# Reordering the opening of a state-space block fused with a gated feed-forward: inputs ahead of weights, own products ahead of the weight decoding

## The chip, the cores and the metric

The kernel runs on one core of a Trainium2 chip. The metric is the time of one execution on the device, in microseconds. A core has a matrix engine (TensorE, PE in the profile; the loading of its stationary operand is listed apart as PEld), a vector engine (VectorE, DVE), an activation engine (ScalarE, ACT), a general engine (GpSimd, POOL) and a sync engine (SyncE, SP) that in this kernel issues every DMA transfer. Each engine runs its own instructions in the order of the program and waits on semaphores for the others. Instructions of the matrix engine write to PSUM[...]; every bank is a named buffer that has to be free before it is written again.

## What is computed

Two stages. The first is a chunked state-space recurrence for 4 batches and 8 heads, 768 steps, head width 32, state width 16; the second a feed-forward with a hard-swish gate on the 3072 rows of 256 values that the first leaves.

```python
# first stage, per batch and head, per chunk of steps (cum is the running sum of log a)
L   = exp(cum[i] - cum[j])  for i >= j, else 0
M   = (C @ B.T) * L
y   = M @ x  +  (C @ state) * exp(cum)
state = exp(cum[last]) * state + sum_j B[j] x[j].T * exp(cum[last] - cum[j])
# second stage
h = y @ w_in                     # 256 -> 2048
g = h * clip(h + 3, 0, 6) / 6
out = g @ w_out                  # 2048 -> 256
```

The kernel works through six blocks (chunks) of 128 steps, each with 4 x 128 = 512 rows. The weights arrive as double precision (64 bits) and are decoded on the chip into float32: they come in eight pieces of 1 MB, four of w_in and four of w_out, numbered 0 to 7 as raws[i].

## The kernel before: the parts that the change touches

The decoding of one piece is a generator; each `weights(i, n)` advances it by n steps. The line numbers of the profile are put beside the operations.

```python
def decode(i):
    ...
    nc.scalar.copy(out=s, in_=top)                     # L199 ACT: sign and exponent bits
    def significand():
        nc.vector.tensor_scalar(out=m, in0=hi, ...)    # L202 DVE
        yield
        nc.vector.scalar_tensor_tensor(out=m, in0=lo, in1=m, ...)  # L206 DVE
        yield
    parts_m = significand()
    if i < 2:
        next(parts_m)
        next(parts_m)
    yield
    nc.vector.tensor_scalar(out=e, in0=s, ...)         # L216 DVE
    nc.vector.tensor_scalar(out=s, in0=s, ...)         # L218 DVE
    next(parts_m, None)
    yield
    nc.scalar.activation(e, e, AF.Relu, bias=bias_hi, ...)   # L222 ACT
    yield
    nc.scalar.activation(e, e, AF.Relu, bias=bias_lo, ...)   # L224 ACT
    next(parts_m, None)
    if i and i + NRAW < 2 * NP:
        load_w(i + NRAW)
    yield
    nc.vector.tensor_tensor(out=e, in0=e, in1=s, op=ALU.bitwise_or)  # L229 DVE
    nc.vector.scalar_tensor_tensor(out=dst, in0=m, in1=e, ...)       # L237 DVE: writes w_in or w_out
```

The steps of the first stage, cut to what is moved:

```python
def diff_mask(c, b):   # L337 PE: starts the differences of chunk c, batch b with the causal mask
def diff(c, *bs):      # L349 and L358 PE: adds cum[i] - cum[j]
def diff_exp(c, b):    # L366 ACT: L = exp(differences)
def turn_b(c):         # L423 PE: four transposes of B, then an ACT copy (L432) to bT
def ends(c, b):        # L397 POOL: B times the decay to the end of the chunk
def scores(c):
    ...                # banks cb0 to cb3 (tags f0 to f3) and y0, y1
    for b in range(NB):            # L523 PE, 64 products: cb <- C, B
        ...
    into_state(c, 0, 1)            # L535 PE, 64 products: y banks <- x, B (what goes into the state)
def multiply(c):
    take(c)                        # L551 ACT: adds <- y
    if c == 0:
        ...                        # L559 ACT, twice: mid <- y (the state in the middle of the chunk)
    for q in range(NQ):
        ...                        # L564 DVE, four times: L <- L * cb[q]
def mix(c):
    for u in range(2):
        ...                        # L589 PE, 64 products: y <- L, x (own products)
        if c == 0:
            from_state(c, 1, ...)  # L501 PE, 16 products: y <- C, mid (from the state)
def keep(c):                       # L603 ACT, four times: yT <- y
def mlp_in(k, f):                  # L611 PE: h <- yT, w_in ; then L689 ACT, L694 DVE
def busy(n, bank):                 # L491 PE: n products of the identity, whose result nobody reads
```

The opening in order of the program:

```python
    load_w(0)
    load_bc(0)      # C in eight transfers of 256-byte runs, then B in one of 64-byte runs
    load_x(0)
    ...
    for c in range(2):
        for b in range(NB):
            diff_mask(c, b)
    ...
    in_three()                       # L277 to L281 DVE: cum split in three bfloat16 parts
    for b in range(2):
        mask_again(0, b)             # L344 PE: 128x512, only to fill the wait
    diff(0, 0, 1)
    diff(0, 2, 3)
    turn_squares(bcs[0][0], turned(0)[2])   # L466 DVE: C turned
    part_heads(0)                           # L473 DVE, twice
    for b in range(NB):
        diff_exp(0, b)
    first_eto()                             # L372 PE, L377 ACT
    weights(0, 1)
    add_up(ends_at[1])                      # L270 DVE
    store_rows()
    diff(1, 2, 3)
    turn_b(0)
    for b in range(NB):
        ends(0, b)
    weights(0, 1)
    diff(1, 0, 1)
    diff_exp(1, 2)
    diff_exp(1, 3)
    weights(0, 2)
    scores(0)
    multiply(0)
    load_w(1, behind=Ls[0][:, 0, 2, :1])    # waits until L <- L * cb[1] is done
    load_w(2)
    load_w(3)
    c_ps = ...; turn_cum(c_ps); by_token(c_ps)
    busy(1, ...)
    fade(0, HALF[1])                        # L479 DVE
    weights(0, 1)
    mix(0)
    keep(0)
    weights(1, 2)
    renew(0)
    weights(1, 3)
    load_eto(1)
    load(1)
    ...
    for f in range(NF):                     # block 0, first product
        mlp_in(k, f)
        for i in weave.get(f, []):
            weights(i, 1)
        if f in (6, 8):
            diff_exp(c, f // 2 - 3)
```

Of the kernel before, what the change touches and what calls it, by code (L numbers as in the profile page):

```python
# [8 lines left out]
FP32 = mybir.dt.float32  # L9
# [4 lines left out]
ALU = mybir.AluOpType  # L14
# [6 lines left out]
def kernel(  # L21
# [63 lines left out]
    def load_bc(c):  # L85

        sl = slice(c * P, (c + 1) * P)

        def tokens_first(src, **where):
            t = loads.tile([P, NB * NH, N], FP32, **where)
            nc.sync.dma_start(out=t, in_=src[:, :, sl, :].rearrange("b h s n -> s (b h) n"))
            return t

        def pairs_first(src):
            t = loads.tile([P, 2, NB, 4, N], FP32, name="pairs", tag="bc")
            for b in range(NB):
                for h in range(2):
                    nc.sync.dma_start(  # L100
                        out=t[:, h, b].rearrange("s a n -> s (a n)"),
                        in_=src[b, h:NH:2, sl, :].rearrange("h (s a) n -> h s (a n)", a=4))
            return t

        if c == 0:
            bcs[c] = [pairs_first(C)]
        elif c < TURN:
            bcs[c] = [tokens_first(C, name="C", tag="bc")]
        Bs[c] = tokens_first(B, name="B")
        if c < TURN:  # L110
            bcs[c].append(Bs[c])
        else:
            bcs[c] = [pairs_first(C), pairs_first(B)]

    def load_x(c):
        sl = slice(c * P, (c + 1) * P)
        xts[c] = loads.tile([P, NB * NH, D], FP32, name="xt")
        nc.sync.dma_start(out=xts[c], in_=x[:, :, sl, :].rearrange("b h s d -> s (b h) d"))
# [22 lines left out]
        nc.sync.dma_start(out=dst, in_=src)  # L141
        raws[i] = raw

    load_w(0)
    load_bc(0)
    load_x(0)
    nc.scalar.preload_act_table_set("natural_log_exp_and_others")


# [38 lines left out]
    def decode(i):  # L188
# [20 lines left out]
            yield  # L209

        parts_m = significand()
        if i < 2:
            next(parts_m)
            next(parts_m)
        yield
# [1 line left out]
            out=e, in0=s, scalar1=0x7FF0, scalar2=None, op0=ALU.bitwise_and)  # L217
        nc.vector.tensor_scalar(  # L218
            out=s, in0=s, scalar1=0x8000, scalar2=None, op0=ALU.bitwise_and)
        next(parts_m, None)  # L220
        yield
        nc.scalar.activation(e.bitcast(BF16), e, AF.Relu, bias=bias_hi, scale=-8.0)  # L222
        yield
        nc.scalar.activation(e, e.bitcast(BF16), AF.Relu, bias=bias_lo, scale=-1.0)  # L224
        next(parts_m, None)
        if i and i + NRAW < 2 * NP:
            load_w(i + NRAW)
        yield
# [110 lines left out]
            start=True, stop=True)  # L339
        ds[c, b] = d  # L340

    def mask_again(c, b):

        nc.tensor.matmul(  # L344
            out=ds[c, b], lhsT=ident_h, rhs=hide.unsqueeze(1).to_broadcast([P, NH, HT]),
            start=True, stop=True)

    def diff_less(c, b):
        nc.tensor.matmul(  # L349
# [64 lines left out]

    def turn_ps(c, j):

        if c < 2:
            return ps.tile([P, NB, P], FP32, name="t_ps", tag=f"f{2 * j if c else 1}")
        return ps_o.tile([P, NB, P], FP32, name="t_ps", tag="o")

    def transposes(c, j, t_ps):
# [23 lines left out]

    def fade_c(c, t_ps):

        nc.vector.tensor_tensor(out=turned(c)[2], in0=t_ps, in1=etos[c], op=ALU.mult)

    def turn(c, j):  # L450
        if j:
# [9 lines left out]
        for b in range(NB):  # L461
            ends(c, b)

    def turn_squares(t, out):

        nc.vector.transpose(  # L466
            out=out.rearrange("r b (s a) -> r b a s", a=4),
            in_=t.rearrange("s t b a n -> s (b a) t n"))

    def part_heads(c):  # L470
        _, cT, csT = turned(c)
        for t in range(2):
            nc.vector.tensor_scalar(  # L473
                out=cT[:, :, t], in0=csT, scalar1=parity[:, t:t + 1], scalar2=None,
                op0=ALU.mult)

    def fade(c, sl=slice(0, P)):
        csT = turned(c)[2][:, :, sl]
        nc.vector.tensor_tensor(out=csT, in0=csT, in1=etos[c][:, :, sl], op=ALU.mult)  # L479

    def turn_all(c):
        bT, _, csT = turned(c)
        for t, out_ in zip(bcs[c], (csT, bT)):
            turn_squares(t, out_)
        part_heads(c)
        fade(c)

    def busy(n, bank):

# [16 lines left out]
    def scores(c):  # L506

        bT, cT, _ = bTs[c]
        cbs[c] = [ps.tile([P, NB, 2, HT], FP32, name="cb", tag=f"f{q}") for q in range(NQ)]
        both = [ps_y.tile([P, 2, NB, HT], FP32, name=f"y{u}", tag=f"y{u}") for u in range(2)]
        ys[c] = {(0, u): both[u][:, 0] for u in range(2)}
        sps[c] = [both[a if c else 1 - a][:, 1] for a in range(2)]
        if c:
            from_state(c, 0)
        for b in range(NB):
            for a, rows in enumerate(HALF):  # L520
                for q in range(NQ):
                    pair = slice(32 * q, 32 * q + 32)
                    nc.tensor.matmul(  # L523
                        out=cbs[c][q][rows, b], lhsT=bT[pair, b, rows],
                        rhs=cT[pair, b, :, rows], start=(b == 0), stop=True,
                        tile_position=(32 * q, a * HT), skip_group_check=True)
        into_state(c, 0, 1)

    def into_state(c, *halves):
        xt, bs = xts[c], bss[c]  # L530
# [22 lines left out]
    def multiply(c):  # L553

        take(c)
        mids[c] = mid = att.tile([P, NB, 2 * D], FP32, name="mid", bufs=1)
        if c == 0:
            for t in range(2):
                nc.scalar.activation(  # L559
                    mid[:, :, t * D:(t + 1) * D], sps[c][0][:, :, t * D:(t + 1) * D], AF.Copy,  # L560
                    scale=parity[:, t:t + 1])
        for q in range(NQ):
            hs = slice(2 * q, 2 * q + 2)
            nc.vector.tensor_tensor(  # L564
                out=Ls[c][:, :, hs], in0=Ls[c][:, :, hs], in1=cbs[c][q], op=ALU.mult)
            if c and q == 1:
                new_state(mid, sps[c][0], tmps[c])

    def renew(c):

# [277 lines left out]
            for b in bs:  # L848
                part(c, b)

    for c in range(2):
        for b in range(NB):
            diff_mask(c, b)
    for sl in ends_at:
        log_a(sl)
    row_signs()
    add_up(ends_at[0])
    in_three()
    for b in range(2):
        mask_again(0, b)  # L860
    diff(0, 0, 1)
    diff(0, 2, 3)
    turn_squares(bcs[0][0], turned(0)[2])
    part_heads(0)
    for b in range(NB):
        diff_exp(0, b)
    first_eto()
    weights(0, 1)
    add_up(ends_at[1])
    store_rows()  # L870
    diff(1, 2, 3)
    turn_b(0)
    for b in range(NB):
        ends(0, b)
    weights(0, 1)
    diff(1, 0, 1)
    diff_exp(1, 2)
    diff_exp(1, 3)
    weights(0, 2)
    scores(0)  # L880
    multiply(0)
    load_w(1, behind=Ls[0][:, 0, 2, :1])
    load_w(2)
    load_w(3)
    c_ps = ps.tile([P, NC, G], FP32, name="c_ps", tag="f1")
    turn_cum(c_ps)
    by_token(c_ps)
    busy(1, ps.tile([P, NB * P], FP32, name="d", tag="f0"))
    fade(0, HALF[1])
    weights(0, 1)  # L890
    mix(0)
    keep(0)
    weights(1, 2)
    renew(0)
# [10 lines left out]
    for k in range(NC):  # L905
        gTs[k] = ffn.tile([P, NF, TB], FP32, name="gT")
        c, ahead = k + 1, k + 2
        if k == 0:
            for f in range(NF):
                mlp_in(k, f)  # L910
                for i in weave.get(f, []):
                    weights(i, 1)
                if f in (6, 8):
                    diff_exp(c, f // 2 - 3)
            load(ahead)
# [119 lines left out]
```

## Time and profile before

| | before |
|---|---|
| median of three runs | 362.05 us (361.94 to 362.84) |
| span of the profiled execution | 361.1 us |
| PE busy | 349.9 us, 97% of the span |
| DVE busy | 223.3 us, 62% |
| ACT busy | 177.2 us, 49% |
| POOL busy | 139.5 us, 39% |
| mean granted clock of PE | 0.989 of full speed |

The busy shares say that the matrix engine is the engine that the whole kernel leans on: what shortens the time has to take away idle or slow time of PE, or work from it. The shares are means over the span, though, and the change touches only the first 40 us or so. That stretch has to be read by itself: from the order of time of the instructions, from the stretches with their granted PE clock, and from the chain of what released what.

### The profile page before, as it was taken

To read this page: it belongs to the slowest core of one execution; us is meant where nothing else is said; L and a number is where in the kernel's file an instruction comes from. 1 tells how busy PE (TensorE), PEld (TensorE's weight loads), DVE (VectorE), ACT (ScalarE), POOL (GpSimd) and SP (SyncE) were. 2 spreads that over 40 slices of the span, in tenths; PEclk is the share of its full clock that TensorE was granted. 3 is DMA by queue.
4 is the path that set the end of the run, shared out by engine and by line. 5 is a ranking of instruction groups with operands and counts; after the bars stand their busy time and mean duration, and the time that the engine had idled before them with its cause. 6 is when DMAs were issued, how large, how long until landed. Compare 5 with 4: busy or idle time off the path is not lost.

```text
span 361.1 us, 9354 instructions
## 1 busy us (share of the span) xinstructions
PE 349.9 (97%) x3936; PEld 300.4 (83%) x3936; DVE 223.3 (62%) x427; ACT 177.2 (49%) x390; POOL 139.5 (39%) x139
## 2 busy tenths in 40 slices
PE   7698999999999999999999999999999999999996
PEld 3553438888888999888999888999888999888996
DVE  4778999976787634587435587535588421588111
ACT  4548878439656550575460476470476110476100
POOL 3400000182299712079722079720058700058700
PEclk9699999999999999999999999999999999999999
DMA  5979969901935043560034560000000000000000
GB/s 154 109 270 254 145 230 156 172 2 43 181 55 77 4 98 91 72 93 2 2 76 104 79 96 2 4 2 31 29 2 1 4 2 31 30 3 0 2 29 31
DMA packets 75482, 24.97 MB, mean 69 GB/s; under 512 B 66032, under 2 KB 71824, under 8 KB 74928
## 3 DMA queue, kind: packets, MB, share of 16 engines
q1 hardware_dynamic: 75440, 24.37, 34.7%
q8 instruction: 31, 0.51, 0.6%
q14 instruction: 11, 0.09, 0.1%
HBM read 21.07 MB, written 3.29 MB: 67 GB/s over the span
## 4 chain that ended last, share of the span: by engine, by line
PE 76%; DVE 13%; ACT 4%; DMA 3%; SPq 2%; issue 1%; DVEq 0%; POOL 0%; ACTq 0%
PE ob L767 18%; PE even L653 18%; PE oa L767 18%; PE odd L653 13%; DVE gT L694 2%; DVE wm L206 2%; PE o L708 2%; PE y L589 2%; PE cb L523 2%; PE y L501 2%; ACT we L222 2%; SPq L100 2%; DMA raw<-in_moe_w_in_dram 2%; DMA B<-in_B_dram 1%; DVE w_out L237 1%; DVE we L229 1%
## 5 line engine op out<-in xcount | busy, mean ns | idle before, releaser
L753 POOL TENSOR_TENSOR s<-gT 128x512 f32<-128x512 f32 x20 | 26.4, 1321 | 89.5 <-DVE gT L694 89.5
L653 PE MATMUL even<-ts,w_sum 128*128 128x256 f32 x160 | 48.2, 383 | 0.0
L668 ACT COPY even<-odd 128x512 f32<-128x512 f32 x40 | 23.0, 576 | 48.6 <-PE odd L653 46.3
L689 ACT ACTIVATE gT<-odd,half 128x512 f32<-128x512 f32 x40 | 27.5, 687 | 35.0 <-DVE odd L682 35.0
L653 PE MATMUL odd<-yT,w_in 128*128 128x256 f32 x160 | 41.1, 379 | 0.0
L767 PE MATMUL oa<-w_out,gT 128*128 128x128 f32 x320 | 38.9, 277 | 0.0
L767 PEld LDWEIGHTS oa<-w_out,gT 128*128 128x128 f32 x320 | 38.1, 192 | 0.9
L767 PE MATMUL ob<-w_out,s 128*128 128x128 f32 x320 | 37.4, 275 | 0.0
L767 PEld LDWEIGHTS ob<-w_out,s 128*128 128x128 f32 x320 | 36.5, 192 | 0.0
L653 PEld LDWEIGHTS even<-ts,w_sum 128*128 128x128 f32 x160 | 29.9, 190 | 5.3 <-ACT up L675 1.5
L694 DVE SCALAR_TENSOR_TENSOR gT<-gT,odd 128x512 f32<-128x512 f32 x40 | 27.5, 688 | 9.9 <-ACT gT L689 9.9
L653 PEld LDWEIGHTS odd<-yT,w_in 128*128 128x128 f32 x160 | 30.1, 190 | 3.9
L386 ACT ACTIVATE L<-L,cum_n 128x64 f32<-128x64 f32 x128 | 31.1, 339 | 0.0
L767 PE MATMUL ob<-t,gT 128*128 128x128 f32 x240 | 30.3, 279 | 0.0
L611 PE MATMUL h<-yT,w_in 128*128 128x512 f32 x64 | 28.4, 599 | 1.9 <-DVE gT L694 1.6
L689 ACT ACTIVATE gT<-even,half 128x512 f32<-128x512 f32 x40 | 27.7, 694 | 4.4 <-PE even L653 4.4
L694 DVE SCALAR_TENSOR_TENSOR gT<-gT,even 128x512 f32<-128x512 f32 x40 | 27.1, 679 | 4.4 <-ACT gT L689 4.4
L767 PEld LDWEIGHTS ob<-t,gT 128*128 128x128 f32 x240 | 27.9, 192 | 1.2 <-issue 0.5
L708 PE MATMUL o<-w_out,gT 128*128 128x256 f32 x128 | 28.7, 381 | 0.0
L669 DVE COPY up<-odd 128x256 f32<-128x256 f32 x40 | 17.0, 424 | 18.7 <-ACT even L668 17.9
L708 PEld LDWEIGHTS o<-w_out,gT 128*128 128x128 f32 x128 | 24.0, 190 | 4.0 <-ACT gT L689 0.8
L397 POOL TENSOR_TENSOR bs<-B,L 128x128 f32<-128x128 f32 x24 | 14.5, 612 | 31.6 <-ACT L L386 23.5
(130 smaller groups left out, 614.9 us busy)
## 6 DMA issues: line engine op xcount, KB each, us to landing
raw<-in_moe_w_in_dram SPq DMA_DIRECT2D x4, 1024.0 KB
raw<-in_moe_w_out_dram SPq DMA_DIRECT2D x4, 1024.0 KB
L<-cum_d SPq DMA_DIRECT2D x8, 512.0 KB
xt<-in_x_dram SPq DMA_DIRECT2D x6, 512.0 KB
out_dram<-res SPq DMA_DIRECT2D x20, 128.0 KB
B<-in_B_dram SPq DMA_DIRECT2D x6, 256.0 KB
eto<-cum_e SPq DMA_DIRECT2D x20, 64.0 KB
pairs<-in_C_dram SPq DMA_DIRECT2D x32, 32.0 KB
```

The source lines that it names most:

```text
L100: nc.sync.dma_start(out=t[:, h, b].rearrange("s a n -> s (a n)"), in_=src[b, h:NH:2, sl, :].rearrange("h (s a) n -> h s (a n)", a=4))
L386: nc.scalar.activation(Ls[c][:, b, h], Ls[c][:, b, h], AF.Exp, bias=cum_n[:, c, g:g + 1])
L397: nc.gpsimd.tensor_tensor(out=bss[c][:, hs], in0=Bs[c][:, hs], in1=Ls[c][:, b, :, HT - 1:HT].to_broadcast([P, NH, N]), op=ALU.mult)
L611: nc.tensor.matmul(out=h.rearrange("p r i -> p (r i)"), lhsT=w_in[:, j, f * P:(f + 1) * P], rhs=yTs[k][:, j].rearrange("p b i -> p (b i)") ...
L653: nc.tensor.matmul(out=bank[:, r], lhsT=lhsT, rhs=rhs, start=start, stop=True, skip_group_check=True)
L668: nc.scalar.copy(out=even, in_=odd[:, 1:2].to_broadcast([P, 2, 2 * P]))
L669: nc.vector.tensor_copy(out=up[:, 1], in_=odd[:, 0])
L689: nc.scalar.activation(gTs[k][:, f], h.rearrange("p r i -> p (r i)"), AF.Relu, bias=half, scale=1.0 / 6.0)
L694: nc.vector.scalar_tensor_tensor(out=g, in0=g, scalar=1.0, in1=h.rearrange("p r i -> p (r i)"), op0=ALU.min, op1=ALU.mult)
L708: nc.tensor.matmul(out=o[:, b % 2], lhsT=gTs[0][:, f, b * P:(b + 1) * P], rhs=w_out[:, f], start=(f == 0 and b % 2 == 0), stop=True, skip_ ...
L753: nc.gpsimd.tensor_tensor(out=o, in0=p_, in1=q_, op=op)
L767: nc.tensor.matmul(out=bank[:, slot], lhsT=lhs[:, j], rhs=rhs[:, j], start=(clear and j == 0), stop=True, skip_group_check=True)
```

## The change

It rearranges the opening so that the data of the first chunk arrive first and the first block's own work runs ahead of the weights.

- The loads go out in the order a, C, B, x, weights 0, in place of a, weights 0, C, B, x. C comes in one transfer of 64-byte runs, as B does, and is turned by four PE transposes, in place of one DVE transpose of 32 x 32 squares.
- The decoding of weight piece 0 moves behind the first multiplications of L with the scores, so that its loading and decoding lie beside them. The significand of piece 0 is now worked out late in its generator.
- The sums for the state (into_state) are put into banks of their own, after the scores, and the ACT steps on them stand between the two ACT steps of the decoding.
- Of the differences of chunk 1, those of batches 0 and 1 move out of the opening into block 0's first product, after f = 2. Ten short mask products (128x192) fill PE's wait in place of two long ones, and three `busy` products stand ahead of the first product in place of one ahead of `mix`.
- The loading of weights 1 is held until the last multiplication of L (it was the second of four).

```diff
-        if c == 0:
-            bcs[c] = [pairs_first(C)]
-        elif c < TURN:
+        if c < TURN:
             bcs[c] = [tokens_first(C, name="C", tag="bc")]
...
-    load_w(0)
     load_bc(0)
     load_x(0)
+    load_w(0)
...
         parts_m = significand()
-        if i < 2:
+        if i == 1:
             next(parts_m)
             next(parts_m)
...
-        next(parts_m, None)
+        if i > 1:
+            next(parts_m, None)
         yield
...
         nc.scalar.activation(e, e.bitcast(BF16), AF.Relu, bias=bias_lo, scale=-1.0)
-        next(parts_m, None)
+        for _ in range(1 if i else 2):
+            next(parts_m, None)
...
-        into_state(c, 0, 1)
+        if c:
+            into_state(c, 0, 1)
...
+    def first_state():
+        sps[0] = [ps_o.tile([P, NB, 2 * D], FP32, name="sp", tag="o") for _ in range(2)]
+        into_state(0, 0, 1)
+        take(0)
+        mids[0] = mid = att.tile([P, NB, 2 * D], FP32, name="mid", bufs=1)
+        for t in range(2):
+            nc.scalar.activation(
+                mid[:, :, t * D:(t + 1) * D], sps[0][0][:, :, t * D:(t + 1) * D], AF.Copy,
+                scale=parity[:, t:t + 1])
...
-    for c in range(2):
-        for b in range(NB):
-            diff_mask(c, b)
+    for b in range(NB):
+        diff_mask(0, b)
+    for b in range(2, NB):
+        diff_mask(1, b)
...
-    for b in range(2):
-        mask_again(0, b)
+    for _ in range(10):
+        mask_again(1, 2, 0)
     diff(0, 0, 1)
+    t_ps = turn_ps(0, 0)
+    turn_c(0, t_ps)
     diff(0, 2, 3)
-    turn_squares(bcs[0][0], turned(0)[2])
-    part_heads(0)
     for b in range(NB):
         diff_exp(0, b)
     first_eto()
-    weights(0, 1)
+    turn_b(0)
+    diff(1, 2, 3)
+    fade_c(0, t_ps)
     add_up(ends_at[1])
-    store_rows()
-    diff(1, 2, 3)
-    turn_b(0)
     for b in range(NB):
         ends(0, b)
-    weights(0, 1)
-    diff(1, 0, 1)
     diff_exp(1, 2)
     diff_exp(1, 3)
+    scores(0)
+    for q in range(3):
+        times_scores(0, q)
     weights(0, 2)
-    scores(0)
-    multiply(0)
-    load_w(1, behind=Ls[0][:, 0, 2, :1])
+    times_scores(0, 3)
+    load_w(1, behind=Ls[0][:, 0, 6, :1])
     load_w(2)
+    store_rows()
+    weights(0, 1)
+    first_state()
+    weights(0, 1)
     load_w(3)
-    c_ps = ps.tile([P, NC, G], FP32, name="c_ps", tag="f1")
+    mix(0)
+    weights(0, 1)
+    c_ps = ps.tile([P, NC, G], FP32, name="c_ps", tag="f2")
     turn_cum(c_ps)
     by_token(c_ps)
-    busy(1, ps.tile([P, NB * P], FP32, name="d", tag="f0"))
-    fade(0, HALF[1])
-    weights(0, 1)
-    mix(0)
+    busy(3, ps.tile([P, NB * P], FP32, name="d", tag="f3"))
     keep(0)
...
                 for i in weave.get(f, []):
                     weights(i, 1)
+                if f == 2:
+                    for b in range(2):
+                        diff_mask(c, b)
+                    diff(c, 0, 1)
                 if f in (6, 8):
                     diff_exp(c, f // 2 - 3)
```

In the changed kernel `times_scores(c, q)` is one of the four multiplications of L with the scores (L564 of before), and `turn_c` and `fade_c` are the PE turn of C with its two DVE copies (`cT`) and the DVE product with the decay (`csT`).

## The prediction

> **What bounds the kernel now.** I read the page first: busy shares and the 40 slices.
>
> ```profile
> PE 349.9 (97%) x3936; PEld 300.4 (83%) x3936; DVE 223.3 (62%) x427; ACT 177.2 (49%) x390; POOL 139.5 (39%) x139
> PE   7698999999999999999999999999999999999996
> ```
>
> A slice is 9 us. PE falls short in the first, second and fourth (7, 6 and 8 tenths); from 36 us on it is full. Only the first 36 us can give anything, and what is won there lasts only if PE starts its long run earlier. 2% would be 7.2 us: more than all of PE's idle time in the span (361.1 - 349.9 = 11.2 us) is likely to yield.
>
> Next the order of time up to 36 us: start, duration, instruction, and in brackets the wait ahead of it.
>
> ```profile
> 8.15 3.28 SPq L118 DMA_DIRECT2D xt<-in_x_dram  x1
> 12.79 1.09 PE L423 MATMUL t_ps<-ident,B 128*128 128x128 f32 x4 [2.78 <-DMA B<-in_B_dram]
> 15.65 2.01 PE L523 MATMUL cb<-cT,bT 32*64 32x128 f32 x64
> 17.79 2.48 DVE L564 TENSOR_TENSOR L<-L,cb 128x512 f32<-128x512 f32 x4 [0.74 <-PE cb L523]
> 19.35 1.42 SPq L141 DMA_DIRECT2D raw<-in_moe_w_in_dram  x3
> 21.44 1.23 DVE L237 SCALAR_TENSOR_TENSOR w_in<-wm,we 128x1024 f32<-128x1024 f32 x1
> 23.46 7.13 PE L611 MATMUL h<-yT,w_in 128*128 128x512 f32 x16
> 24.81 0.69 DVE L202 TENSOR_SCALAR wm<-raw 128x1024 uint32<-128x1024 uint32 x1 [2.15 <-DMA raw<-in_moe_w_in_dram]
> 31.44 1.27 DVE L694 SCALAR_TENSOR_TENSOR gT<-gT,h 128x512 f32<-128x512 f32 x2
> ```
>
> PE stands still from 10.0 until B lands. The first product then waits for yT (23.46), not for its weights (done at 22.67). The same view of PE alone, later:
>
> ```profile
> 32.17 14.14 PE L611 MATMUL h<-yT,w_in 128*128 128x512 f32 x32 [1.58 <-DVE gT L694]
> 46.67 7.13 PE L611 MATMUL h<-yT,w_in 128*128 128x512 f32 x16 [0.36 <-DVE w_in L237]
> ```
>
> Before f = 4 PE waits 1.58 us for DVE, which decodes piece 1 (landed 24.81) first. So two chains meet at 32.17 us, the **junction**: PE's, and that of piece 1, whose load is held until L is multiplied. After it PE runs almost without a stop. The change is worth what it moves the junction.
>
> The stretches of 1 us (PE, PEld, DVE, ACT, POOL busy, then PE's granted clock, DMA share, GB/s) show a third cost:
>
> ```profile
> 11.00:12.00 1.00, 0.00 (x0) 0.00 (x0) 0.96 (x2) 0.00 (x0) 0.00 (x0) 1.00 0.43 30
> 12.00:13.00 1.00, 0.21 (x1) 0.24 (x2) 1.00 (x3) 0.00 (x0) 0.20 (x1) 0.51 0.92 145
> 18.00:19.00 1.00, 0.78 (x56) 0.54 (x37) 1.00 (x3) 1.00 (x2) 0.00 (x0) 0.58 0.00 0
> 19.00:20.00 1.00, 0.87 (x5) 0.62 (x6) 1.00 (x3) 0.72 (x3) 0.19 (x1) 1.00 0.00 0
> ```
>
> Two microseconds into the stop the clock falls to half and stays there for 6.8 us, through transposes, differences and scores.
>
> [...] x's data (526 KB moved from 12 to 16 us) follow B's.
>
> **The change part by part.**
>
> Loads. From the stretches: B moved in about 2.3 us (9.3 to 11.6, with latency landing at 12.65); x in 3.4 us (12.0 to 15.4); weights 0 in about 3.4 us (from 2.3). C now has B's form, 262 KB in 64-byte runs. So C: first data 2.4, done 4.7, landed 5.4. B: 0.3 us between, done 7.3, landed about 8. x done 11.0, landed 11.6. Weights 0 done about 13.5, landed T0 = 13.9. (Before they had landed by 9.75, when ACT copies them.) The DVE turn of C (1.08 us) and the wait for C (4.4 us) go.
>
> PE up to the scores. The split is ready at 6.33 as before; until then ten 128x192 masks fill PE. Differences of two batches took 1.17 us (6.34 to 7.5), so: differences 7.5, turn of C 0.6 (four transposes at 69.82) to 8.1, differences 9.3, eto 9.6, turn of B 10.2, differences of chunk 1 11.4. No transfer is late, no stop over 0.5 us, clock full. ACT: two exponentials of L (0.56 each) from 7.35, two from 9.15 to 10.3, eto 10.7, bT 11.3. Scores 11.4 to 12.6 (1.2 us at full clock, at 76.2). They ended at 17.7 before: 5 us earlier. DVE reaches the multiplications of L at 12.6, behind the scan (1.42 us from 11.1); three of them, 0.64 each, end at 14.6.
>
> Then everything hangs on T0. ACT copy of weights 0 (1.12 us): 15.05. L216 and L218 (0.5 each): 16.1; fourth multiplication: 16.75. Weights 1 are issued then: 16.75 + 0.2 (POOL) against 19.35, 2.4 us earlier. Piece 1 takes 24.81 - 19.35 = 5.46 us to land and 32.17 - 24.81 = 7.36 us to the junction: 16.95 + 12.82 = **29.8**, 2.4 us earlier than before.
>
> PE's chain: ACT, in order: L222 1.15 from 15.55, adds 0.37, mid 0.63: 17.75. PE has done the state sums and the first half of mix (by 14.8) and waits for mid for 3 us. Then from_state, second half of mix, from_state, 2.0 us (21.45 to 23.46 before): 19.75; c_ps 0.36: 20.1; three busy products at two passes of 0.43 each: 2.6: 22.7. Weights 0 are ready at 17.75 + L224 1.15 + 0.69 + 1.23 = 20.9 and yT about 20.5, so busy, not the decoding, sets the start: 22.7, 0.8 us earlier. Four f take 7.13, and the moved differences add two masks at 0.21 and 1.17, 1.6 together: 22.7 + 7.1 + 1.6 + 0.1 = **31.5**. It is the later of the two: the junction moves 0.7 us.
>
> The 1.6 us of moved work thus fill the old wait of 1.58. Beyond the junction piece 1's side is now 1.7 us ahead, so the wait of 0.36 at 46.67 and one of 0.54 at 75.2 (PE on csT, behind DVE) can go, perhaps half: 0.4. Sum 1.1 us: 362.05 - 1.1 = 360.9.
>
> **The rivals.**
>
> 1. The clock falls in the wait for mid. [...] a wait of 1.58 us left it full. [...] The rest of mix, c_ps and busy, 3.9 us at full clock, then lose up to 1.6 us, and the junction is at 33: time 362.5 to 363. [...]
>
> 2. busy ends near the first product's own readiness, because mid comes earlier than I reckon or the waits overlap. Then the junction is 29.8 to 30.5: gain 2 to 2.4, time 359.6 to 360.1. For it: someone chose three, and would not if one were enough.
>
> 3. Weights 0 land late (SP's issue of x took 3.28 us with B ahead of it, and now C, B and x stand ahead). A microsecond on T0 is a microsecond on both chains: T0 = 15.5 makes 362.5.
>
> **Range and chances.** Centre 360.9; rivals 1 and 3 pull up, 2 down. 359.4 to 362.8 should hold it 8 times in 10. All lie within 2%: faster by more 0.01, within 0.98, slower by more 0.01.
>
> **What would show it.** Right: no PE stop over 1 us before the state sums, full clock through the scores, and these over by 13; weights 0 landing near 13.9; a PE wait near 3 us for ACT's mid; no wait ahead of f = 4, with DVE ahead of PE there. Wrong: a clock of 0.5 after 15 us, the first product later than 23.5, or earlier than 21.5; a landing later than 15; new PE waits between 32 and 54 us because decoding falls behind.

## The result, and the profile after

The changed kernel takes 366.84 us (median of 4, 366.69 to 368.67) against 362.44 for the kernel before beside it (361.94 to 363.38): a ratio of 1.013, interval 1.009 to 1.0169. It is slower by 4.4 us where 1.1 us of gain was predicted, and outside the range of 359.4 to 362.8. The profiled executions took 366.69 and 362.84 us, with spans of 365.0 and 361.1, so their traces differ by 3.9 us. That is what the traces can explain; the medians differ by 0.5 more because the profiled execution of before lies 0.4 above its median and that of after 0.15 below.

The page of the kernel after, busy shares, the 40 slices (9.1 us each) and the transfers of instructions:

```profile
PE 352.4 (97%) x3952; PEld 303.2 (83%) x3952; DVE 222.2 (61%) x426; ACT 177.7 (49%) x390; POOL 137.4 (38%) x139
PE   7589999999999999999999999999999999999996
PEclk9959999999999999999999999999999999999999
q8 instruction: 31, 0.51, 0.6%
```

PE's row reads 7, 5, 8, 9 where it read 7, 6, 9, 8: the second slice has become emptier. The third slice of the clock row is the 5 that the rest hangs on.

The order of time of the opening after, to set beside the one of before:

```profile
11.02 1.21 PE L514 MATMUL cb<-cT,bT 32*64 32x128 f32 x64
12.29 1.88 DVE L556 TENSOR_TENSOR L<-L,cb 128x512 f32<-128x512 f32 x3 [0.22 <-PE cb L514]
14.40 0.60 PE L527 MATMUL sp<-xt,bs 64*32 64x64 f32 x36 [1.24 <-issue]
16.46 1.09 ACT L196 COPY ws<-raw 128x1024 uint16<-128x1024 uint16 x1 [4.50 <-DMA raw<-in_moe_w_in_dram]
18.39 0.68 DVE L556 TENSOR_TENSOR L<-L,cb 128x512 f32<-128x512 f32 x1
20.03 1.12 PE L492 MATMUL y<-csT,mid 32*64 32x64 f32 x16 [4.39 <-ACT mid L566]
21.78 1.23 DVE L236 SCALAR_TENSOR_TENSOR w_in<-wm,we 128x1024 f32<-128x1024 f32 x1
23.80 4.27 PE L482 MATMUL d<-ident 128*128 128x512 f32 x6
26.14 0.69 DVE L199 TENSOR_SCALAR wm<-raw 128x1024 uint32<-128x1024 uint32 x1 [1.94 <-DMA raw<-in_moe_w_in_dram]
27.91 5.31 PE L612 MATMUL h<-yT,w_in 128*128 128x512 f32 x12
```

The scores are over at 12.2 us instead of 17.7: that half of the change does what it was made for. Then ACT waits 4.50 us for weights 0 (16.46), PE waits 4.39 us for ACT's mid (20.03), and the filler `busy` (L482) runs from 23.80, although w_in was ready at 21.78 + 1.23 = 23.01 and yT at 23.73. The first product starts at 27.91 us. Before, it started at 23.46.

The stretches of 1 us after (PE, PEld, DVE, ACT, POOL busy, then granted clock, DMA share, GB/s):

```profile
15.00:16.00 1.00, 0.65 (x64) 0.48 (x46) 0.00 (x0) 0.00 (x0) 0.00 (x0) 1.00 0.13 41
16.00:17.00 1.00, 0.00 (x0) 0.00 (x0) 0.00 (x0) 0.54 (x1) 0.00 (x0) 0.74 0.00 0
17.00:18.00 1.00, 0.00 (x0) 0.00 (x0) 0.42 (x1) 0.55 (x1) 0.00 (x0) 0.50 0.00 0
26.00:27.00 1.00, 1.00 (x2) 0.30 (x2) 0.76 (x2) 0.86 (x1) 0.00 (x0) 0.64 1.00 371
27.00:28.00 1.00, 1.00 (x4) 0.47 (x3) 1.00 (x1) 0.30 (x1) 0.00 (x0) 1.00 1.12 415
```

Through transposes and scores, where before had half clock, the clock is now full. It falls at 16.5 us, 0.8 us after PE has run dry, and comes back at 26.7: 10.2 us at half. No weight bytes move between 16 and 20 us, as weights 1 aren't released yet. Of the 41 KB of the stretch from 15 to 16 us, 25 are the end of weights 0 (the other 16 are a transfer of instructions that starts at 15.77), and these are late by themselves: from 14.94 us on the packets of 4 KB come one after the other, 0.16 us each, and the last ends at 15.99. While x and weights 0 were coming in, from 11.4 to 13.0 us, the queue of instructions moved this (number, MB, share of 16 engines):

```profile
q8 instruction: 1, 0.02, 5.9%
```

5.9% of 16 engines over 1.6 us is one DMA engine for 1.5 us (11.47 to 12.98). Experiment 9 comes back to it.

PE alone past the junction:

```profile
34.64 22.58 PE L612 MATMUL h<-yT,w_in 128*128 128x512 f32 x52
57.06 15.70 PE L709 MATMUL o<-w_out,gT 128*128 128x256 f32 x72
```

Both waits of before (1.58 at 32.17, 0.36 at 46.67) are gone. The 52 products start with f = 3, so f = 4 starts four products later, at 36.46 us by the trace. The output product starts at 57.06, where before it started at 53.77.

**How the loss is measured from here on.** In both traces the first product of each later block starts at a clear point (before: 86.5, 142.4, 197.1, 251.8, 306.3 us). A kernel's *opening lag* is how much later than before it passes the three points from 142.4 to 251.8; its *late loss* is what the last point adds. After: 2.8 and 1.0, sum 3.8, and the spans differ by 3.9. The late loss lies in one place, the last block's scores. PE alone there, the kernel after:

```profile
288.37 0.86 PE L527 MATMUL y<-xt,bs 64*32 64x64 f32 x64
289.16 0.38 PE L768 MATMUL ob<-t,gT 128*128 128x128 f32 x1
290.10 1.83 PE L768 MATMUL ob<-t,gT 128*128 128x128 f32 x15 [0.56 <-issue]
```

and the same of the kernel before:

```profile
285.27 0.86 PE L535 MATMUL y<-xt,bs 64*32 64x64 f32 x64
286.06 2.05 PE L767 MATMUL ob<-t,gT 128*128 128x128 f32 x16
```

The kernel after stops one product into a row of sixteen, for a reason that no semaphore shows ("issue"); the kernel before goes through. The diff touches nothing within 250 us of it.

### The profile page after: what moved, and what is told of

Its sections match the earlier page's. It is cut to its first block, busy times and chain, and to the rows that moved or that the text cites. A ratio compares the mean times of both kernels' runs of the same rounds, so it can differ in the third digit from the quotient of the medians.

```text
span 365.0 us, 9373 instructions
## 1 busy us (share of the span) xinstructions
PE 352.4 (97%) x3952; PEld 303.2 (83%) x3952; DVE 222.2 (61%) x426; ACT 177.7 (49%) x390; POOL 137.4 (38%) x139
## 4 chain that ended last, share of the span: by engine, by line
PE 86%; SPq 4%; DVE 3%; DMA 3%; ACT 2%; issue 1%; DVEq 0%; ACTq 0%
PE ob L768 18%; PE oa L768 17%; PE even L654 15%; PE odd L654 12%; PE o L709 8%; PE h L612 8%; DMA raw<-in_moe_w_in_dram 3%; PE y L590 2%; PE y L492 2%; SPq L99 2%; PE cb L514 1%; PE d L482 1%; PE y L527 1%; SPq L92 1%; SPq L115 1%
## 5 line engine op out<-in xcount | busy, mean ns | idle before, releaser
L612 PE MATMUL h<-yT,w_in 128*128 128x512 f32 x64 | 27.9, 594 | 0.0
L404 POOL TENSOR_TENSOR tmp<-state,eto 128x256 f32<-128x256 f32 x5 | 3.3, 658 | 62.0 <-DMA eto<-cum_e 54.7
```

Source lines behind the costliest of these rows:

```text
L612: nc.tensor.matmul(out=h.rearrange("p r i -> p (r i)"), lhsT=w_in[:, j, f * P:(f + 1) * P], rhs=yTs[k][:, j].rearrange("p b i -> p (b i)") ...
```

## Experiments

Two questions were open: what of the opening lag comes from which cause (half clock, the filler, late weights), and what stops PE at 290 us. The times below were measured with the kernel before run beside each group (its medians 362.44 to 363.38, so ratios compare better than times); PE instructions count a product and its operand load as two, so after has 2 x (3952 - 3936) = 32 more than before.

| kernel | PE instructions over before | opening lag, us | late loss, us | time, us | ratio to before |
|---|---|---|---|---|---|
| after | +32 | 2.8 | 1.0 | 366.84 | 1.013 (1.009 to 1.0169) |
| no_busy | +20 | 2.1 | 0.9 | 365.51 | 1.0057 (1.0037 to 1.0076) |
| fill | +52 | 0.9 | 2.3 | 366.33 | 1.0084 (1.0058 to 1.011) |
| fill_no_busy | +40 | 1.0 | 1.8 | 365.59 | 1.0067 (1.0048 to 1.0086) |
| w_before_x | +32 | 2.75 | 1.5 | 367.04 | 1.0113 (1.0083 to 1.0142) |
| before_narrow | +32 | -0.6 | 1.2 | 363.36 | 1.0004 (0.9993 to 1.0014) |
| before_wide | +8 | 0.55 | 0.0 | 362.73 | 0.9992 (0.9976 to 1.0007) |
| no_busy_wide | +4 | 0.4 | 0.3 | 364.37 | 1.0036 (1.0024 to 1.0047) |
| best_try | +16 | 0.6 | 0.3 | 362.87 | 0.9997 (0.9982 to 1.0011) |
| own_first | +40 | -1.7 | 1.7 | 362.85 | 0.9995 (0.9981 to 1.0009) |
| own_first_short | +16 | 1.6 | 0.5 | 364.82 | 1.0037 (1.0024 to 1.005) |
| own_first_three | +16 | 0.0 | 0.65 | 363.78 | 1.0028 (1.0018 to 1.0039) |
| own_first_wide | +24 | -1.8 | 1.2 | 362.35 | 1.0006 (0.9984 to 1.0029) |

pad20 and pad40 have PE stops elsewhere too and stand only in the text. Lags come from one profiled execution each, ratios from all. The profiled execution of before had a mean granted clock of 0.989; 100 of the 148 executions of it beside the experiments had 0.994 or 0.995, so the lags may flatter the others by some tenths of a us. In fill, 0.4 of the late loss falls before the point at 251.8. All these kernels do the whole of the work; they differ in order and in products that nobody reads.

**1. no_busy: the filler after the mix taken away.** From after:

```diff
-    busy(3, ps.tile([P, NB * P], FP32, name="d", tag="f3"))
```

> The changed kernel without its three busy products. Theory: they lie on PE's own path at half clock (23.8 to 27.5 us of the trace), because weights 0 were ready at 23.0 and yT at 23.7; without them the first product starts at 23.8, runs at half clock until about 26.7 and loses 1.5 us there, so f = 4 starts at about 34.0 in place of 36.4: 2.3 us faster than the changed kernel, about 2 us slower than before. Rival: busy only fills a wait for the decoding, then nothing moves (4.4 us slower than before). Second rival: without busy the clock stays at half for longer, then the time is no better or worse than the changed kernel's.

Its first product, PE alone:

```profile
23.75 8.34 PE L612 MATMUL h<-yT,w_in 128*128 128x512 f32 x12
```

The product starts 4.2 us earlier, but takes 8.34 us for what took 5.31: the clock is half from 16.0 to 29.7 us now. The filler had cost 4.1 us (23.80 to 27.91); without it the half clock falls on the product, and the opening lag falls by 0.7 only. The median is 2.5 us over the 362.98 of before beside it, where after's was 4.4 over. The medians gain more than the trace because the length of the half clock differs between executions: of no_busy's eight, three had a mean granted clock of 0.980 or 0.981, the profiled one among them (365.76 to 366.49 us), and five had 0.984 to 0.986, as after's profiled one (364.24 to 365.52).

**2. fill: the wait for mid filled with five identity products.** From after, in `mix(0)` between the first half of the own products and the product with mid:

```diff
             if c == 0:
+                if u == 0:
+                    busy(5, ps.tile([P, NB * P], FP32, name="d", tag="f2"))
                 from_state(c, 1, (2 * u, 2 * u + 1))
```

> The changed kernel with five more products of the identity (4.3 us at full clock) placed in PE's wait for mid, between the first half of mix and from_state; the three busy products stay. Theory: the half clock from 16.5 to 26.7 us costs by itself; with PE kept at work the clock stays full, from_state, mix, c_ps and busy take 5 us in place of 7.5, the first product starts near 25.0 in place of 27.5 and f = 4 near 33.7: 2.5 us faster than the changed kernel, about 1.7 us slower than before. Rival (the late weights alone are the cause, the clock costs nothing): no change, 4.4 us slower than before. If the fillers run past the arrival of mid: slower than that by what they run over.

PE alone: the new filler, the old one, the first product.

```profile
15.54 4.56 PE L482 MATMUL d<-ident 128*128 128x512 f32 x10
22.39 2.84 PE L482 MATMUL d<-ident 128*128 128x512 f32 x6
25.07 5.31 PE L614 MATMUL h<-yT,w_in 128*128 128x512 f32 x12
```

The clock stays full throughout (mean granted clock 1.0, in after 0.985) and the first product starts at 25.07, 2.8 us earlier than after's 27.91. The opening lag falls by 1.95, so the half clock is shown to cost that. The median is still 3.35 us over the 362.98 of before, because the late loss has grown from 1.0 to 2.3.

**3. fill_no_busy: both edits together.**

> Both: five fillers in the wait for mid, no busy products. Theory: PE is done with the attention work at 22.4 us at full clock and waits for weights 0 (23.0) and yT; the first product starts near 23.1, PE would reach f = 4 at 31.9, but the decoding of piece 1 frees the bank only at 33.4 (as in the changed kernel's trace, 34.05 less its own lateness). So 1.2 us slower than before, 3.2 us faster than the changed kernel; what is left is the late landing of weights 0. Rival (the moved differences are the rest): PE has no wait ahead of f = 4.

PE alone at the first product and at f = 4, and DVE at the landing of piece 1:

```profile
23.28 5.39 PE L614 MATMUL h<-yT,w_in 128*128 128x512 f32 x12 [0.65 <-DVE w_in L236]
33.37 14.14 PE L614 MATMUL h<-yT,w_in 128*128 128x512 f32 x32 [1.30 <-DVE gT L697]
26.00 0.69 DVE L199 TENSOR_SCALAR wm<-raw 128x1024 uint32<-128x1024 uint32 x1 [2.67 <-DMA raw<-in_moe_w_in_dram]
```

With filler and half clock out of the way, the old junction is back, with a wait of 1.30 for DVE at f = 4, and it stands at 33.37, 1.2 us later than before, because piece 1 lands at 26.00 instead of 24.81. So the floor under after's opening lag, 1.0 us, is piece 1.

**4. w_before_x: weights 0 issued ahead of x.** From after:

```diff
     load_bc(0)
-    load_x(0)
     load_w(0)
+    load_x(0)
```

> The changed kernel with weights 0 issued ahead of x (order C, B, weights 0, x). Theory: weights 0 land near 11.5 us in place of 16.4 and x near 15 in place of 12.7; the state sums wait for x, mid is there at 17 in place of 20.0, and the first product starts at 22.0 if the clock stays full (f = 4 at 30.8: 1.3 us faster than before), or near 24.5 if it falls to half in the wait for x (1 to 1.5 us slower than before). Rival (order of loads does not matter, busy and clock alone do): 4.4 us slower than before.

PE alone, the state sums and the filler:

```profile
16.15 0.85 PE L527 MATMUL sp<-xt,bs 64*32 64x64 f32 x64 [3.47 <-DMA xt<-in_x_dram]
22.73 5.31 PE L482 MATMUL d<-ident 128*128 128x512 f32 x6
```

Now x is last, at 16.15, where weights 0 were at 16.46. PE waits 3.47 us one step earlier, the clock is half from 17.5 to 27.7, and the opening lag is the same (2.75). The order of these two does not matter: what lands last comes at about 16 us either way.

**5. before_narrow and before_wide: only PE's instruction count changed, in the kernel before.** Ahead of `turn_b(0)`, where PE waits for B:

```diff
+    for _ in range(16):                  # before_narrow: 32 instructions
+        nc.tensor.matmul(out=ds[1, 0][:, :3], lhsT=ident_h,
+            rhs=hide.unsqueeze(1).to_broadcast([P, 3, HT]), start=False, ...)
+    busy(2, ps.tile([P, NB * P], FP32, name="d", tag="f3"))   # before_wide: 8, instead
```

> The kernel before with 16 narrow mask products (128x192, each with its own weight load: 32 PE instructions, about 1.7 us) in PE's wait for B at 10.0 us; they add zeros or the mask to masked places, the output is unchanged. Two theories are read apart in one trace. Opening: the clock stays full through 19 us (it fell to half at 12.0), the multiplications of L are bound by DVE's decoding (17.05) and f = 4 starts 0.5 to 1 us earlier than 32.17. Late loss: if the extra 1 us that all variants of the changed kernel lose between 285 and 293 us comes from where in PE's program its instruction fetches fall, then 32 more instructions (as many as the changed kernel has more than before) bring it here too: a PE stop of 0.5 to 1.5 us near 290 us that nothing releases. Rival (the loss belongs to the changed opening): no stop there.

> The kernel before with two products of the identity over 512 columns (8 PE instructions, 1.7 us) in the same wait. Opening as with the 16 narrow ones: full clock, f = 4 earlier by 0.5 to 1 us. Fetch theory: 8 instructions move the fetches by little, the stop near 290 us is under 0.4 us, and the kernel is 0.5 us faster than before. Rival (a stop near 290 follows from an earlier junction): a stop as with the narrow ones.

before_narrow, PE alone near 286 us:

```profile
284.65 0.86 PE L535 MATMUL y<-xt,bs 64*32 64x64 f32 x64
285.43 0.38 PE L767 MATMUL ob<-t,gT 128*128 128x128 f32 x1
286.84 1.83 PE L767 MATMUL ob<-t,gT 128*128 128x128 f32 x15 [1.03 <-issue]
```

This is the kernel before with 32 instructions added 270 us earlier, and it has after's stop, at the same product. With 8 added there is none, and no late loss. So the late loss belongs to no part of the change: 32 more instructions ahead of it are enough. It doesn't hang on an early opening either: after has the stop with a lag of 2.8, before_narrow with -0.6. What the stop waits for is not shown. A hint is in the transfers of the stretch from 284.5 to 286 us in before_narrow (queue: number, MB, share of 16 engines):

```profile
q8 instruction: 1, 0.02, 3.9%
```

One transfer of instructions of 16 KB lies here; 3.9% of 16 engines over 1.5 us is 0.94 us of one engine, and it ends at 285.46, when the row has just begun and PE is about to stop. The transfer alone does not stop PE: the kernel before has one from 285.04 to 286.09 and goes through. What has to come together with it no run isolates.

The same pair says what half clock had cost the kernel before: with a full clock all along (before_narrow, mean granted clock 1.0 for 0.989) the opening is 0.6 us ahead, and the late stop takes it back.

**6. no_busy_wide and best_try: fewer, wider fillers.** The ten 128x192 masks of the opening become two of 128x512, and the filler goes (no_busy_wide, from after); best_try does this on w_before_x and puts three identity products into the wait for x.

```diff
-    for _ in range(10):
-        mask_again(1, 2, 0)
+    for _ in range(2):
+        nc.tensor.matmul(out=ds[1, 2], lhsT=ident_h,
+            rhs=hide.unsqueeze(1).to_broadcast([P, NH, HT]), start=False, ...)
...
+        busy(3, ps_o.tile([P, NB * P], FP32, name="d", tag="o"))   # best_try, in first_state
-    busy(3, ps.tile([P, NB * P], FP32, name="d", tag="f3"))
```

> The changed kernel without busy and with two wide mask products in place of ten narrow ones: its PE program ahead of the late blocks is 4 instructions longer than that of before, where no_busy had 20. Fetch theory: the opening lag is that of no_busy (2 us at the last block's scores) and the loss between 284 and 293 us falls from 0.9 to under 0.3 us: 2.0 to 2.3 us slower than before in all. Rival: the late loss stays at 0.9, 3 us slower.

> The changed kernel with weights 0 ahead of x, no busy products, three products of the identity (2.6 us) in the wait for x, two wide masks in place of ten narrow ones: 16 PE instructions more than before. Theory of the opening (half clock, busy, and the load of weights 1 hanging on weights 0): the clock stays full, x is there at 16, mid at 17.8, PE ends mix at 19.9, weights 0 are decoded at 20.9, first product 21.0; weights 1 land at 21.7; f = 4 at 29.8: 2.4 us earlier than before. Late loss by the fetch theory 0.6 to 0.9. In all 1.5 us faster than before. Rival (something else of the changed opening costs): f = 4 later than 31.

no_busy_wide does as the count says: late loss 0.3 with 4 more instructions than before. Its opening lag of 0.4 against no_busy's 2.1 was not expected and lies in the length of the half clock as far as the traces show: both are at half from about 16 us, for 13.7 us in no_busy's profiled execution and for 10.2 us (16.7 to 26.9) here. best_try missed its gain for a reason not expected. PE alone, second half of the own products:

```profile
18.48 0.34 PE L591 MATMUL y<-L,xt 64*32 64x64 f32 x14
20.66 1.06 PE L591 MATMUL y<-L,xt 64*32 64x64 f32 x50 [1.85 <-issue]
```

An "issue" stop of 1.85 us in the opening, and from 19.95 on, 1.1 us into it, 6.8 us of half clock. This execution took 363.89 us with a mean granted clock of 0.989; 15 of the 20 had 0.994 to 1.0 and a median of 362.77, so it shows one way to lose the gain and not the usual length of the half clock.

**7. pad20 and pad40: best_try with 20 or 40 tiny masks in place of its two wide ones (36 and 76 instructions more).**

```diff
-    for _ in range(2):
+    for _ in range(20):      # pad40: 40
         nc.tensor.matmul(
-            out=ds[1, 2], lhsT=ident_h, rhs=hide.unsqueeze(1).to_broadcast([P, NH, HT]), ...)
+            out=ds[1, 2][HALF[0], 0], lhsT=ident_h[:, HALF[0]], rhs=hide, ...)
```

> best_try with 20 tiny products (40 PE instructions) in place of the two wide masks: 36 PE instructions more ahead of the state sums. Fetch theory: the stop that stood after 28 products' instructions of the second half of mix (18.8 to 20.7 us) comes 36 instructions earlier, that is at the end of from_state's first half, and lasts about as long (1.5 to 1.9 us). Rival (the stop is a wait on some buffer or engine): it stays where it is.

> best_try with 40 tiny products (80 PE instructions) in place of the two wide masks: 76 PE instructions more. Fetch theory: [...] no stop between 16 and 21 us, the clock stays full, first product near 21.2, f = 4 near 30: 2 us earlier than before. The late loss is open, 0.3 to 2 us. If the stop only moves (to mix's first half) without getting shorter: f = 4 at 32 as in best_try.

pad20 and pad40, PE alone at the stop:

```profile
18.25 0.56 PE L492 MATMUL y<-csT,mid 32*64 32x64 f32 x12 [0.34 <-ACT mid L567]
22.27 0.47 PE L492 MATMUL y<-csT,mid 32*64 32x64 f32 x4 [3.46 <-issue]
```

```profile
11.65 1.19 PE L514 MATMUL cb<-cT,bT 32*64 32x128 f32 x63
15.74 0.32 PE L514 MATMUL cb<-cT,bT 32*64 32x128 f32 x1 [2.90 <-issue]
```

Count back from the stop of best_try, which lies behind the first 16 products with mid and 14 of the next own products, together 60 instructions. pad20 stops 12 products in, at 24: moved by 36, exactly what was added. pad40 stops one product before the end of the scores. Between there and best_try's stop lie 1 + 64 + 6 + 64 + 30 = 165 products (scores, state sums, filler, own products, the 30 just counted), 330 instructions; 76 were added, and 254 are left. An estimate from the page of after, 2 x 3952 PE instructions over the 31 transfers of queue q8, is 255 to a transfer, if all 31 carry PE's, which the trace doesn't say. So the stop of pad20 moved with the count of the instructions ahead of it, not with a piece of the work; that the one of pad40 is the same stop one transfer earlier is the author's reading of 254 beside that estimate. The expected place in pad20 was right, its length was not (3.46 us for 1.5 to 1.9). In pad40 the hoped-for gain missed: the stop at the end of the scores was not foreseen, and f = 4 stood at 32.5, not near 30. The times were 365.72 (1.0077, 1.0052 to 1.0102) and 365.42 (1.006, 1.0037 to 1.0083).

**8. own_first: piece 1 released early.** fill_no_busy, with the fourth multiplication of L and the loads behind it put ahead of the decoding of piece 0:

```diff
-    for q in range(3):
+    for q in range(4):
         times_scores(0, q)
-    weights(0, 2)
-    times_scores(0, 3)
     load_w(1, ...)
     load_w(2)
+    weights(0, 2)
```

> The changed kernel with full clock and without busy (five fillers in the wait for mid), and with the fourth multiplication of L and the loads of weights 1 and 2 moved ahead of the decoding of weights 0. Theory: what is left of the lag in fill_no_busy (f = 4 at 33.37, 1.2 us after before) is that weights 1 were issued at about 19.7 us because the fourth multiplication stands behind DVE steps that wait for weights 0 (landed 16.4). Moved ahead, weights 1 are issued at about 15.1 and land by 19.5 [...]; piece 1 is then decoded in time, the wait ahead of f = 4 goes, the first product stays at 23.3 and f = 4 starts at 32.0: the lag at the late blocks falls from 1.0 to about -0.2 us. The late loss stays at 1.5 to 1.9 us, in all 1.5 us slower than before. Rival (piece 1 hangs on the order of the decoding steps, not on its load): f = 4 stays at 33.4.

PE alone, the first product, the one after the moved differences, and the late stop:

```profile
23.29 5.39 PE L614 MATMUL h<-yT,w_in 128*128 128x512 f32 x12 [0.67 <-DVE w_in L236]
30.09 4.13 PE L614 MATMUL h<-yT,w_in 128*128 128x512 f32 x9
285.81 0.30 PE L527 MATMUL y<-xt,bs 64*32 64x64 f32 x3 [1.14 <-issue]
```

The wait at f = 4 is gone and the clock is full from 7 us on (mean granted clock 1.0): the opening is 1.7 us *ahead* of before, 2.7 better than fill_no_busy, where 1.2 had been expected. This shows that piece 1 was held by the place of its release, on DVE behind two decoding steps (17.72 and 18.18 in fill_no_busy, then the multiplication at 18.52). The late loss of 1.7 takes the gain back.

**9. own_first_short, own_first_three, own_first_wide: own_first with fewer PE instructions, to keep its opening without the late stop.** Five fillers become four and all masks go (short); three fillers and two wide masks (three); five fillers and two wide masks (wide).

> own_first with four fillers in place of five and none of the ten narrow masks: 16 PE instructions more than before ahead of the late blocks, where own_first has 40. Fetch theory: the loss between 284 and 293 us falls from own_first's 1.7 to about 0.3 us (best_try, also 16 more, lost 0.28), while the opening keeps most of own_first's gain of 1.7: about 1.3 us faster than before. Rival (the late loss comes with an early junction and not with the number of instructions): loss stays at 1.7, no faster than before.

> own_first with three fillers in place of five and two wide masks in place of ten narrow ones: also 16 instructions more than before. Late loss as in own_first_short, 0.3 us. The fillers end near 18.3 us and leave PE idle for 1.9 us until mid: if the clock then falls to half, the opening gains 0.5 us or less; if it stays full, 1.7. In all 0.2 to 1.4 us faster than before.

> own_first with two wide masks in place of the ten narrow ones and all five fillers: 24 PE instructions more than before, where own_first has 40. The clock stays full from 7 us on, the opening keeps own_first's gain (1.5 to 1.7 us). Fetch theory: the late loss is between those seen at 20 (0.9) and 16 (0.3 to 0.7) and that at 32 (1.0): 0.5 to 1.0 us. In all 0.6 to 1.2 us faster than before. Rival: the late loss stays at 1.7, as before in all.

The first two lose the clock. In own_first_short PE waits 1.69 us ahead of its first differences (0.23 in own_first), these take 1.03 us for 0.72, and the clock is full only from 11.2 us; an issue stop of 2.44 us that ends at 17.30 is followed by half clock from 18.0 to 21.4. This run also bears on weights 0. Up to their copy it differs from own_first only in the ten masks that it leaves out, and its instruction transfer falls later (14.82 to 15.82, in own_first 11.62 to 13.10). The stretch from 15 to 16 us and ACT's copy of weights 0:

```profile
15.00:16.00 1.00, 0.00 (x0) 0.00 (x0) 1.00 (x3) 0.39 (x1) 0.00 (x0) 1.00 0.01 4
15.61 1.11 ACT L196 COPY ws<-raw 128x1024 uint16<-128x1024 uint16 x1 [1.59 <-DMA raw<-in_moe_w_in_dram]
```

Of the late 25 KB of weights 0 at most 4 are left, and ACT copies at 15.61, where own_first did at 16.57. In the eight runs with the loads in after's order and the transfer at 11.4 to 13.1 us, the copy stood at 16.36 to 16.58. So about 0.9 us of the lateness of weights 0 goes with the kernel's own instruction transfer. The trace doesn't name DMA engines: that the transfer and the late packets share one is not shown.

In own_first_three the filler ends before mid is there, PE alone:

```profile
19.98 0.68 PE L492 MATMUL y<-csT,mid 32*64 32x64 f32 x16 [1.89 <-ACT mid L566]
```

and half clock follows from 23.4 to 26.8, 3.4 us after this wait of 1.89 has ended. own_first_wide keeps the clock and an opening of -1.8, but still stops late, PE alone:

```profile
286.15 1.39 PE L770 MATMUL ob<-t,gT 128*128 128x128 f32 x11 [0.76 <-issue]
```

Its median of 362.35 against 363.12 is the best of all, but of its 22 executions 15 took 361.5 to 363.6 and 7 took 365.2 to 366.4, and the ratio's interval (0.9984 to 1.0029) includes no change. All 7 had a mean granted clock of 0.994 or 0.995, and 13 of the 15 had 0.998 to 1.0; two with 0.995 took about 363.5, so the half clock is not the whole of it. The rest isn't settled: the profiled execution was one of the 15. No version was shown to beat the kernel before.

## Why the prediction was wrong

**Right.** The loads of C, B and x: no PE stop of over 1 us ahead of the scores, full clock through them, and the scores over at 12.2 ("over by 13"). The order of ACT (L220 at 18.05, adds at 19.10, mid at 19.35, L222 at 19.87) and of DVE was as told, and the moved differences cost 34.64 - 33.06 = 1.58 us of PE (predicted 1.6) and filled the old wait at f = 4. From the first product to the junction 8.6 us passed (36.46 - 27.91; predicted 31.5 - 22.7 = 8.8).

**First failed step: "Weights 0 done about 13.5, landed T0 = 13.9".** ACT could copy them at 16.46, 2.6 us later. Three terms were too small. x's data ended at 11.63 rather than 11.0 (0.6). All but the last packets of the 1 MB took another 3.3 us (to 14.94), not the 2.5 us left between 11.0 and 13.5 (0.8); the prediction's own rate, 3.4 us for the piece, already said more, so this was a slip of the sum. And the last packets came up to 1.05 us behind the others (15.99), which the sum had no term for: about 0.9 of it goes with the instruction transfer from 11.47 to 12.98, going by own_first and own_first_short. From there to ACT's copy 0.5 us passed, for 0.4 allowed. Rival 3 named the lateness, at 15.5, though for another reason, SP's issuing: x was issued by 6.67, and the data of weights 0 began as x's ended. As it said, everything behind T0 moved along: mid's product stood at 20.03, not 17.75 (2.3 us), after a PE wait of 4.39 instead of 3.

**Second failed step: "22.7", the first product, worked out at full clock.** Rival 1 was right that the clock falls in the wait for mid, and too mild: its loss of up to 1.6 us was the author's estimate, and the clock was at half for 10.2 us. It fell at 16.5, only 0.8 us into the wait. Shortly ahead of that lay a second gap, the "issue" stop of 1.24 us in the state sums (14.40), which no step of the prediction knew. From mid to the filler took 3.77 us (20.03 to 23.80) for 2.35 predicted, the filler 4.1 (to 27.91) for 2.6: 1.4 + 1.5 = 2.9 us. fill, with a full clock, moved the first product by 2.8. The sum: 2.3 + 2.9 = 5.2 on the first product, 27.9 instead of 22.7. Rival 2 did not come true: it had the filler end near the first product's own readiness, but the operands were ready at 23.7, and the filler held PE until 27.9. Yet no_busy alone recovered only 0.7 us of lag, as without it the product itself ran at half clock.

**The other chain, "29.8".** Weights 1 were to be issued at 16.95, and landed at 26.14 instead of 16.95 + 5.46 = 22.4: they were released at 19.71 and took 6.4 us. The fourth multiplication, which releases them, stands on DVE behind two steps of piece 0's decoding (17.58 and 18.05), so it ran at 18.39. In the changed kernel the later PE chain hides this; fill_no_busy uncovered it (1.0 us behind before), and own_first, which moves only this step, gained 2.7.

**"Perhaps half: 0.4".** The lag was 36.46 - 32.17 = 4.3 at the junction, 57.06 - 53.77 = 3.3 at the output product, 3.1 at the first product of block 1 and 2.8 at that of block 2. So 1.5 came back; the two named waits explain 0.36 + 0.54 of it, the rest wasn't traced.

**What the prediction did not see at all: 1.0 us at 290 us.** "After it PE runs almost without a stop" holds for the kernel before, not for a PE stream 32 instructions longer. before_narrow, with 32 instructions added and nothing of the change, has the same stop (1.03 us).

**The sum.** Predicted: -0.7 at the junction, -0.4 behind it. Found: +4.3, -1.5, +1.0, together 3.8 of the 3.9 us between the profiled spans. The opening's 2.8 cannot be split into fixed shares: full clock alone takes away 1.95, no filler alone 0.7, both 1.85, because each hides the other, and piece 1 is the 1.0 underneath.

## What to carry to other kernels

Getting the small inputs in early only moved the stop here to whatever was loaded last (at about 16 us in after and in w_before_x): before a reorder, add up all bytes ahead of the last load, and ask who waits for it and how long the matrix engine will then stand without work. The program's own instructions are bytes too: here a 16 KB transfer of them went with 0.9 us on a 1 MB load. A load should be released by the earliest step that frees its buffer, not one queued behind decoding that waits for another load (own_first: 2.7 us of the opening). A kernel that lives on long runs of small products should be compared over its whole length after any change of instruction count, as an opening can be paid for 270 us later (before_narrow: 0.6 us ahead, then a late loss of 1.2).

## What was not expected of the hardware

**PE stopped where the profile shows nothing to wait for, and in one pair of runs the place moved with the instruction count.** Stops of 0.6 to 3.5 us with the releaser "issue" came in dense stretches of small products (the scores and state sums, 256 instructions in about 2 us); from best_try to pad20 the stop moved by 36 instructions, as many as were added. In four of the stops PE started again 1.3 to 1.6 us after the end of a 16 KB instruction transfer (after: 12.98 to 14.40 and 288.8 to 290.10; before_narrow: 285.46 to 286.84; best_try: 19.09 to 20.66). That PE waits for its instructions there is the author's reading and was not shown: the kernel before has such a transfer up to 286.09 and no stop. Late losses grew roughly with the instructions added (0.3 at +4, 0 at +8, 0.3 to 0.65 at +16, 1.0 to 1.5 at +32, 2.3 in fill and 1.9 in pad20 at +52). How to keep a stop out of a dense stretch isn't shown.

**The clock fell to half near PE's stops, and the length of a stop alone does not tell when.** In before it fell at 12.0 us, 2.0 us into the wait for B of 2.78, and in after at 16.5, 0.8 us into the wait for mid of 4.39. In w_before_x it fell at 17.5, 1.4 us after the wait for x of 3.47 had ended, and in own_first_three at 23.4, 3.4 us after a wait of 1.89. Other stops left it full: 1.58 us at 32.17 in before, 1.23 in fill (mean granted clock 1.0), and 2.90 in pad40:

```profile
PEclk9999999999999999999999999999999999999999
```

The half clock lasted 3.4 us in own_first_short and own_first_three, 6.8 in before and best_try, 10.2 in after, w_before_x and no_busy_wide, and 13.7 in no_busy. What sets its start and its length isn't shown. The same kernel can also have half clock for a different time in each execution (experiment 1).

**More filler is not more clock for free.** Five identity products of 0.91 us each hold the clock in the wait (fill, mean granted clock 1.0), but each is four instructions, and with these 20 the late loss went from 1.0 to 2.3 us.
